# Forgetting attention and a gated feed-forward: a joined score bank, weights in three chunks, additive masks for batch 0, and a new stored order

## The chip, the cores and the metric

One core of a Trainium2 chip runs the whole kernel in one launch. The engines work side by side: PE (TensorE, matrix products and transposes), DVE (VectorE), ACT (ScalarE), POOL (GpSimd) and SP (SyncE, which issues transfers here). Each follows its own stream of instructions, and they meet at semaphores. The metric is the time of one execution on the device, in microseconds (us); lower is better.

## What is computed

There are B = 8 batches, H = 8 heads, S = 576 positions, head size D = 64. The attention decays with distance: the score of query i and key j has the sum of the logarithms of the forget gates between them added. Its output, 4608 rows of 512, goes through a root-mean-square norm and a gated feed-forward of width 1536.

```python
scores = scale * np.matmul(q, k.transpose(0, 1, 3, 2))
cum = np.cumsum(np.log(np.clip(f, 0.0001, 1.0)), axis=-1)
scores = np.where(causal, -1e9, scores + cum[..., :, None] - cum[..., None, :])
attn = softmax(scores); x = (attn @ v) as rows of H * D
xn = x / np.sqrt(np.mean(x * x, axis=-1, keepdims=True) + 1e-06) * rms_g
g = xn @ w_gate
out = (g * sigmoid(g) * (xn @ w_val)) @ w_out
```

(The second line and the line of the softmax are shortened.)

## The kernel before

The kernel is a list of small *pieces*, each a few instructions for one engine, registered by `plan.add` under a name. The string ORDER, stored at the top of the file, names all of them in one sequence. `Plan.run` walks it and issues each piece to its engine; so ORDER sets the order within each engine, and the engines run apart as far as data and buffers allow. `*n` after a name asks for n filler matmuls (L235, `warm_up`) that compute nothing, ahead of that piece's own; `:ff` picks the PSUM pool for a product of values.

The decay isn't added to scores. The exponential of minus the cumulated gates is folded into V and into a 65th column of V that collects the denominator, so a division at the end gives the attention.

The names, where b is a batch, p one of four pairs of heads, g a group of rows:

- `Lq`, `Lk`, `Lqk`, `Lv` (L388 to L400, L431) load 256 KB pieces of q, k and v (128 or 64 KB for the last 64 rows), all from SP's queue. `Cq`, `Ck`, `Cqk` (L412) cast them to bf16, nearly all on POOL. `Sv` (L419 to L426) scales v.
- `tr`, `trt` (L491 to L521) turn q and k on PE in batches 0 to 2; `keeptr` (L508, L513, L524) copies the result out of PSUM. `tk`, `tq`, `tt` (L552, L555) are DMA transposes from batch 3 on.
- `sc` (L620) computes one or two banks of scores of a pair into a tile of 2 × 512 columns (two heads side by side), of which there are two. `esc` (L628) takes the exponential on ACT into a tile PT, and `msc` (L636) zeroes the part above the diagonal on POOL. `k4`, `sc4`, `exp4`, `mask4` (L580, L589, L593, L597) do the last 64 rows.
- `val` (L656) multiplies by V; `xpo` (L665, L666) divides by the denominator into x. `sq` (L673, ACT), `ms` (L679, DVE), `rs` (L684, POOL) and `xn` (L688, DVE) are the norm. `xtr`, `kxtr` (L715 to L724) turn x on PE in batches 0 and 1; `tx` (L707) does so by DMA later.
- `g`, `v` with a suffix f (L811) are the gate and value matmuls, `th` (L816) a tanh on ACT, `ga`, `hga` (L820, L827) the gating on DVE, `pj` (L837) the projection in two parts, `o` (L842) the copy out of PSUM, `so` (L845) the store, from POOL's queue except in the last group.
- `wg`, `wv` (L352, four chunks each) and `wo` (L364, two) load the weights from POOL's queue.

The rows are taken in ten groups: two of 256 rows (g0, g1), then eight of 512. The first 256 positions of batch 0 are a part of their own (HEAD), so that g0 can begin; the rest of batch 0 (REST) has three banks a pair, and batches 1 to 7 (WHOLE) three banks a pair with all 576 positions. Each bank is a list of blocks: (key block, first query, queries, column in the tile).

Buffers: 10 for loads, 6 for cast operands, 4 PT, two score tiles, one PSUM bank for values, three PSUM banks `ff` shared by gate, value, projection and transposes. ORDER puts the feed-forward of a group among the attention of the batches that follow.

Of the kernel before, what the change touches and what calls it, by code (L numbers as in the profile page):

```python
# [16 lines left out]
NB = 5  # L17
# [17 lines left out]
g0.6 exp4.1 Lk2.0 hga0.4 sc1.0.1024 keeptr1.3.q th0.6 xtr0.3 Lq2.3 v0.6f ga0.6 kxtr0.3 xn0.4 esc1.1.0 xtr0.2 Lqk20 g0.8 kxtr0.2 hga0.6 g1.0 th0.8
esc1.0.1024 ga0.8 v1.0f Sv1.0 Lk2.1 th1.0 sc1.1.512 ga1.0 g1.2 esc1.1.1024 Lq2.0 hga1.0 v0.8f th1.2 esc1.1.512 Lk2.3 ga1.2 g0.10 hga0.8 v1.2f
msc1.1.1024 th0.10 ga0.10 sc1.2.0 mask4.1 esc1.2.0 xtr0.4 g1.4 Sv1.4 kxtr0.4 hga1.2 esc1.2.512 v1.4f th1.4 msc1.0.1024 Lq2.1 v0.10f ga1.4 Sv1.2
sc1.2.1024 hga1.4 g1.6 esc1.3.0 hga0.10 Sv1.3 v1.6f th1.6 esc1.2.1024 ga1.6 g1.8 Lqk21 Sv1.1 v1.8f th1.8 ga1.8 sc1.3.512 esc1.3.512 val1.0.0 hga1.6
Lk2.2 val1.1.0:ff hga1.8 esc1.3.1024 g1.10 pj0.0.0 msc1.3.1024 th1.10 ga1.10 msc1.2.1024 Lv2.3 xpo1.1.0 Lv2.41 xpo1.0.0 val1.2.0:ff Ck2.0 val1.4.0:ff
xpo1.2.0 Lv3.41 pj0.0.0e Cq2.0 xpo1.4.0 val1.5.0 o0.0.0 val1.3.0:ff Ck2.1 Lq2.2 xpo1.5.0 val1.6.0:ff Ck2.3 Lk3.0 xpo1.3.0 tr2.0 Cq2.1 val1.7.0 Lqk31  # L40
xpo1.6.0 keeptr2.0.k Cqk2 tr2.1 Lk3.3 keeptr2.0.q pj0.1.0 Cq2.3 keeptr2.1.k Lq3.3 xpo1.7.0 keeptr2.1.q sq1.1 Lv2.40 Sv2.3 sq1.2 Lq3.0 pj0.1.0e so0.0.0
v1.10f o0.1.0 Ck2.2 Lq3.1 sq1.4 trt2 sc2.0.0 keeptrt2 sq1.0 Cq2.2 hga1.10 tr2.3 Lqk30 sq1.3 k4.2 tr2.2 pj1.0.0 Lv2.0 ms1.0 keeptr2.2.k keeptr2.2.q
rs1.0 esc2.0.512 keeptr2.3.q Lq3.2 keeptr2.3.k xn1.3 sc4.2 pj1.0.0e xn1.0 exp4.2 xtr1.3 o1.0.0 pj1.1.0 xn1.1 kxtr1.3 xn1.2 esc2.0.0 xn1.4 xtr1.0
xtr1.1 kxtr1.0 pj1.1.0e kxtr1.1 xtr1.2 sc2.0.1024 kxtr1.2 Cq3.0 esc2.0.1024 xtr1.4 g2.0 kxtr1.4 tq3.0 o1.1.0 Cq3.1 v2.0f th2.0 Cqk3 esc2.1.0 Lv2.1
ga2.0 g2.1 Cq3.3 tq3.1 hga2.0 Ck3.3 v2.1f th2.1 Ck3.0 ga2.1 sc2.1.512 Lv2.2 mask4.2 esc2.1.512 g2.2 hga2.1 Lq4.3 msc2.0.1024 v2.2f tk3.0 th2.2 Sv2.0
esc2.1.1024 ga2.2 g2.3 Lk4.0 hga2.2 Cq3.2 v2.3f th2.3 Lk3.1 Sv2.1 ga2.3 sc2.2.0 tt3 g2.4 esc2.2.512 hga2.3 Sv2.2 tq3.2 v2.4f th2.4 Sv2.4 esc2.2.0
# [85 lines left out]
class Plan:  # L132
# [779 lines left out]
```

The softmax here doesn't subtract the row's maximum and nothing guards it: scores larger than these inputs give would overflow.

## Time and profile before

| | us |
|---|---|
| median of 5 executions | 384.13 |
| lowest and highest | 382.42, 384.77 |
| the profiled execution, its own time | 384.13 |
| its span, first to last instruction | 382.1 |
| ACT, all exponentials of scores (L628) | 96.8 |
| PE, gate and value matmuls (L811) | 110.1 + 109.7 |
| PE, projection (L837) | 97.2 |
| POOL, casts (L412) | 43.9 |
| POOL, masks (L636) | 37.6 |
| POOL, store issues (L845) | 18.4 |

The span is what the trace covers; 2.0 us of the profiled execution's own time lie outside it. Matmuls overlap in PE's pipeline, so the sum of their durations is somewhat above the time in which PE works. The busy time of an engine says how full it is, and not whether anything waited for it.

### The profile page before, as it was taken

What the parts mean: (1) busy time and instruction counts of PE and PEld (TensorE: products, weight loads), DVE (VectorE), ACT (ScalarE), POOL (GpSimd) and SP (SyncE); (2) the same over time, 40 slices, a digit from 0 to 9 for tenths busy, and PEclk for the clock granted to TensorE, in tenths of its full rate; (3) what the DMA queues carried; (4) which work ended last, traced back from release to release, by engine and by line L of the source; (5) the groups of instructions that cost most, each with busy time, mean ns of one, the idle gap of its engine ahead of it and who ended that gap; (6) DMA issues with size and microseconds to landing.
All of it is one profiled execution on the core that took longest, in us unless ns stands there. A gap on an engine that the chain in (4) does not pass through costs nothing.

```text
span 382.1 us, 8426 instructions
## 1 busy us (share of the span) xinstructions
PE 366.3 (96%) x3270; PEld 203.3 (53%) x3314; DVE 246.4 (64%) x460; ACT 215.0 (56%) x357; POOL 174.3 (46%) x281
## 2 busy tenths in 40 slices
PE   8679899989999999999999999999999999999996
PEld 7457787744654644454445544554444544444443
DVE  4656875776777776467855877487348845743750
ACT  2667786578687568346655496556554353313322
POOL 4667626878398537793664359224111221001000
PEclk9989999999999999999999999999999999999999
DMA  8999997799779999999997964830001224022002
GB/s 204 187 260 236 233 237 161 166 205 174 165 159 221 157 190 196 207 197 179 222 171 121 205 143 102 118 107 13 14 30 21 84 69 98 1 62 84 0 6 107
DMA packets 144840, 52.62 MB, mean 138 GB/s; under 512 B 128220, under 2 KB 142304, under 8 KB 144800
## 3 DMA queue, kind: packets, MB, share of 16 engines
q1 hardware_dynamic: 136336, 38.82, 53.7%
q0 software_dynamic: 8384, 13.11, 15.1%
q8 instruction: 26, 0.43, 0.5%
q10 hardware_dynamic: 80, 0.15, 0.1%
q14 instruction: 14, 0.11, 0.1%
HBM read 37.90 MB, written 9.44 MB: 124 GB/s over the span
## 4 chain that ended last, share of the span: by engine, by line
PE 85%; DVE 5%; ACT 4%; DMA 3%; SPq 2%; issue 1%; ACTq 0%; DVEq 0%
PE ff L811 49%; PE ff L837 22%; PE sc L620 6%; PE po L656 4%; PE ff L656 3%; DMA st<-in_v_dram 2%; ACT junk L673 1%; DVE xn L688 1%; DVE x L666 1%; ACT PT L628 1%; SPq L431 1%; DMA xT<-xn 1%; ACT QK L513 1%; DVE QK L513 1%; PE sc L235 1%
## 5 line engine op out<-in xcount | busy, mean ns | idle before, releaser
L820 DVE SCALAR_TENSOR_TENSOR ga<-th,ff 128x512 f32<-128x512 f32 x108 | 74.1, 686 | 66.6 <-ACT th L816 65.0
L628 ACT ACTIVATE PT<-sc 128x1024 bf16<-128x1024 f32 (+2 forms) x100 | 96.8, 990 | 29.8 <-PE sc L620 29.8
L811 PE MATMUL ff<-xT,wg 128*128 128x512 bf16 (+1 forms) x467 | 110.1, 357 | 1.0 <-DMA xT<-xn 0.2
L811 PE MATMUL ff<-xT,wv 128*128 128x512 bf16 (+1 forms) x464 | 109.7, 357 | 0.8
L816 ACT ACTIVATE th<-ff 128x512 f32<-128x512 f32 x108 | 64.5, 597 | 72.6 <-PE ff L811 67.4
L837 PE MATMUL ff<-wo,hT 128*128 128x512 bf16 (+1 forms) x429 | 97.2, 373 | 0.7
L827 DVE SCALAR_TENSOR_TENSOR hT<-ga,ff 128x512 bf16<-128x512 f32 x108 | 73.8, 685 | 7.9 <-PE ff L811 0.2
L636 POOL TENSOR_SCALAR_AFFINE_SELECT PT<-PT 128x1024 bf16<-128x1024 bf16 (+1 forms) x44 | 37.6, 865 | 77.0 <-ACT PT L628 76.3
L811 PEld LDWEIGHTS <-wg 128*128 128x128 bf16 x480 | 44.7, 98 | 43.4 <-issue 1.9
L811 PEld LDWEIGHTS <-wv 128*128 128x128 bf16 x480 | 45.1, 98 | 42.4 <-issue 1.0
L837 PEld LDWEIGHTS <-hT 128*128 128x128 bf16 x444 | 42.2, 98 | 46.4 <-issue 1.1
L412 POOL CAST ld<-st 128x512 bf16<-128x512 f32 x68 | 43.9, 668 | 24.5 <-DMA st<-in_q_dram 9.7
L842 ACT COPY ores<-ff 128x512 f32<-128x512 f32 (+1 forms) x37 | 21.0, 574 | 48.6 <-PE ff L837 41.4
L688 DVE SCALAR_TENSOR_TENSOR xn<-x,rs,rgb 128x512 bf16<-128x512 f32 x40 | 37.2, 959 | 6.9 <-POOL rs L684 6.8
L656 PEld LDWEIGHTS <-PT 128*128 128x128 bf16 x896 | 33.5, 98 | 12.3 <-issue 2.9
L845 POOL DMA_DIRECT2D out_dram<-ores x32 | 18.4, 576 | 39.6 <-ACT ores L842 39.6
L419 POOL TENSOR_TENSOR Vs<-st,decT 128x512 bf16<-128x512 f32 x27 | 29.0, 1076 | 9.4 <-DMA st<-in_v_dram 9.0
L620 PE MATMUL sc<-QK 64*128 64x128 bf16 (+2 forms) x328 | 28.6, 270 | 1.2 <-DVE QK L508 1.0
L673 ACT ACTIVATE junk<-x 128x512 bf16<-128x512 f32 x40 | 25.1, 628 | 3.1 <-DVE x L666 2.6
L620 PEld LDWEIGHTS <-QK 64*128 64x128 bf16 x584 | 15.8, 95 | 18.4 <-issue 13.3
L656 PE MATMUL po<-Vs,PT 128*128 128x65 bf16 x521 | 22.3, 194 | 1.8 <-DVE Vs L420 1.8
L666 DVE TENSOR_TENSOR x<-po,rden 128x320 f32<-128x320 f32 (+2 forms) x39 | 18.6, 478 | 1.3
(84 smaller groups left out, 232.0 us busy)
## 6 DMA issues: line engine op xcount, KB each, us to landing
st<-in_k_dram SPq DMA_DIRECT2D x32, 256.0 KB, 4.7
st<-in_q_dram SPq DMA_DIRECT2D x32, 256.0 KB, 4.4
st<-in_v_dram SPq DMA_DIRECT2D x32, 256.0 KB, 4.4
out_dram<-ores POOLq DMA_DIRECT2D x32, 256.0 KB, 3.0
wo<-in_moe_w_out_dram POOLq DMA_DIRECT2D x2, 768.0 KB, 14.2
st<-in_k_dram SPq DMA_DIRECT2D x8, 128.0 KB, 4.5
st<-in_q_dram SPq DMA_DIRECT2D x8, 128.0 KB, 5.6
st<-in_v_dram SPq DMA_DIRECT2D x16, 64.0 KB, 4.3
```

Of the source, the lines that this page charges most:

```text
L412: {"DVE": nc.vector.tensor_copy, "POOL": nc.gpsimd.tensor_copy, "ACT": nc.scalar.copy}[eng](o, x)
L419: e.tensor_tensor(Vs[i][:, j, :, 0:D], t, bcast(dj, D), ALU.mult)
L620: nc.tensor.matmul(sc[:, par, c:c + n], lhsT=k_cols(r, p, kj), rhs=q_cols(r, p, q0, n), start=True, stop=True)
L628: nc.scalar.activation(T["pt", b, p][:, :, c0:c0 + n], T.pop(("sc", b, p, c0))[:, :, 0:n], ACT.Exp, scale=scale)
L636: nc.gpsimd.affine_select(out=d, in_=d, pattern=[[0, m], [1, 128]], compare_op=ALU.is_ge, fill=0.0, base=0, channel_multiplier=-1)
L656: nc.tensor.matmul(T["po", b, hs][:, qm, m, :], lhsT=w, rhs=Vs[i][:, kj, h, :], start=(kj == 0), stop=(kj == qi))
L688: nc.vector.scalar_tensor_tensor(xn, in0=T["x", b][:, j, :], scalar=T["rs", b, js][:, j:j + 1], in1=rgb, op0=ALU.mult, op1=ALU.mult)
L811: nc.tensor.matmul(ps[:, c * w:c * w + w], lhsT=wt[:, dc, (fc + c) * 128:(fc + c + 1) * 128], rhs=T["xT", g][:, dc, 0:w], start=(dc == 0), ...
L816: nc.scalar.activation(t, T["pg", g, fc], ACT.Tanh, scale=0.5)
L820: nc.vector.scalar_tensor_tensor(a, in0=T.pop(("th", g, fc)), scalar=1.0, in1=T.pop(("pg", g, fc)), op0=ALU.add, op1=ALU.mult)
L827: nc.vector.scalar_tensor_tensor(o, in0=T.pop(("ga", g, fc)).rearrange("p (c t) -> p c t", t=w), scalar=0.5, in1=T.pop(("pv", g, fc)).rear ...
L837: nc.tensor.matmul(po, lhsT=T["hT", g][:, fc, j * 128:(j + 1) * 128], rhs=wo[:, fc, c0:c1], start=(fc == 0), stop=(fc == NFC - 1))
```

## The change

*Joined bank.* The blocks of key block 0 in batches 1 to 7, of 128 and 384 queries, become one of 512; that bank is computed first (suffix 512), and the one of suffix 0 after it.

*Masks.* For batch 0, `msc` goes. A piece `far` opens the PSUM tile with a product of the identity and a constant triangle of −30000, and the score matmuls add to it. For batches 1 to 7, one select over 1024 columns becomes three.

*Batch 0's last small banks* (suffix 384) of all four pairs share one score tile and one visit.

*Weights* come in three chunks per matrix. *x* has fixed tiles with one more column that holds a constant, so that the square's sum has the epsilon in it, and `ms` goes. *Fillers* go in runs of 512 columns, and their number is another: 176 of 128 columns before, 81 units of 128 after.

*Engines.* A mark `@` in ORDER names the engine of a piece (A is ACT, D DVE, O POOL, S SP). 24 casts go to ACT and 13 to DVE; 16 loads are issued by ACT instead of SP; 12 output copies go to DVE; of the stores, 8 go to ACT, 11 to SP and three of the last group to POOL; four of the eight `k4` leave POOL.

*Dependence.* `expo` and every `esc` now follow `fetch`, the piece that fetches the exponential's table.

*Order.* The whole string is another. Below it is cut to the head, up to the first gate piece, and to the start of the last group.

```diff
-one lf ident Lk0.0 Lq0.1 rg identb clear Lk0.1 Lq0.0 Lq0.2 Lqk11 Lk0.2 clip turn_rg*48 keep_rgT Lqk00 Ck0.0 fetch_ln spread_rg*3 Lv0.0 Cq0.1 log scan
-Lv0.1 Cq0.0 Ck0.1 tr0.01*29 tr0.00 Cq0.2 Lk0.3 keeptr0.00.k keeptr0.00.q keeptr0.01.k expo Lqk01 keeptr0.01.q tr0.02*7 sc0.1.0 keeptr0.02.q Lv0.40
-esc0.1.0 twice keeptr0.02.k Lq0.3 Ck0.2 sc0.2.0*5 msc0.1.0 turn_dec esc0.2.0 Lv0.3 sc0.0.0 tr0.03 keep_rg msc0.2.0 keeptr0.03.k Lk1.0 keeptr0.03.q
-Lv0.41 keep_dec sc0.3.0*8 wv0 tr0.10 esc0.3.0 Sv0.1 Lq1.0 wg1 esc0.0.0 Ck0.3 Lv1.40 Sv0.0 fetch msc0.0.0 Lv0.2 keeptr0.10.q val0.2.0*16 Lk1.2 xpo0.2.0
-msc0.3.0 val0.0.0:ff*5 sc0.1.512 xpo0.0.0 val0.4.0 esc0.1.512 Cqk0 xpo0.4.0 val0.6.0:ff Cq0.3 xpo0.6.0 Lq1.2 Ck1.0 tr0.12*8 Lk1.1 sq0.1 sc0.0.512 wg0
-Lq1.3 keeptr0.12.q keeptr0.10.k trt0 sq0.0 keeptrt0 sc0.3.512*1 esc0.3.512 ms0.0 rs0.0 keeptr0.12.k sc0.2.512*10 wv1 xn0.0 esc0.2.512 Sv0.3 wg2
-sc0.1.1024*10 k4.0 xn0.1 Lq1.1 xtr0.0 esc0.1.1024 Lqk10 tri esc0.0.512 kxtr0.0 Lv1.41 xtr0.1*9 Sv0.2 sc0.2.1024 Cq1.0 kxtr0.1 sc4.0 Sv0.4 esc0.2.1024
-Lk1.3 g0.0*1 msc0.1.1024 Lv1.0 sc0.0.1024 th0.0 v0.0f exp4.0 ga0.0 esc0.0.1024 sc0.0.384 g0.2 mask4.0 hga0.0 esc0.0.384 msc0.0.1024 sc0.1.384 tr1.0
...
-hga8.6 v8.7f th8.7 ga8.7 g8.8 hga8.7 v8.8f th8.8 ga8.8 g8.9 hga8.8 v8.9f th8.9 ga8.9 g8.10 hga8.9 v8.10f th8.10 ga8.10 g8.11 hga8.10 v8.11f th8.11
-xn7.4 pj8.0.0 ga8.11 tx7.4.9 xn7.1 hga8.11 tx7.1.9 pj8.0.0e pj8.1.0 o8.0.0 tx7.3.9 so8.0.0 pj8.1.0e pj8.2.0 pj8.2.0e pj8.3.0 o8.2.0 o8.1.0 so8.2.0
...
+one lf far Lq1.0 Lq0.0 Lq0.1@A ident Lk0.0 Lv0.1@A tri identb clear Lk0.1 Lq0.3@A fetch_ln rg Lk0.2 clip Lk0.3@A log Cq0.1@A scan Lq0.2 Cq0.0@A Lqk01
+fetch Lv0.0 Ck0.0 tr0.01*48 Lqk11@A far0.1.0 keeptr0.01.q tr0.00 keeptr0.01.k far0.3.0 expo keeptr0.00.q sc0.1.0 Ck0.1@D Cq0.3@A twice keeptr0.00.k@D
+tr0.02 Lv0.40 turn_dec esc0.1.0 Lk1.0 tr0.03 turn_rg Ck0.2@O Lqk00@A far0.0.0 keeptr0.03.q keep_rgT keeptr0.03.k sc0.0.0 Lqk10@A Ck0.3 sc0.3.0
+keeptr0.02.k tr0.12 esc0.3.0 keep_dec Lq1.3 Cq0.2 keeptr0.02.q Sv0.1@O Lv0.2@A tr0.10*2 keeptr0.12.q far0.1.1024 esc0.0.0 keeptr0.12.k@D spread_rg
+Cq1.0 Lv0.3 keeptr0.10.k Cqk0@D far0.2.0 keeptr0.10.q sc0.2.0 Lk1.3@A Sv0.0@O trt0 esc0.2.0 Lv0.41 keeptrt0 wv0 sc0.1.1024*6 Cqk1@A val0.0.0 Lk1.2
+val0.4.0:ff keep_rg val0.6.0:ff xpo0.0.0 k4.0 Lk1.1 esc0.1.1024 val0.2.0:ff sc0.0.384 Lq1.2 wg0 xpo0.2.0 esc0.1.384 Lq1.1 sc4.0 xpo0.4.0 wg1 exp4.0
+xpo0.6.0 esc0.3.384 far0.3.1024*4 esc0.0.384 Ck1.0 esc0.2.384 sc0.3.1024 Sv0.2 sq0.0 sc0.1.512 Lv1.41 trt1 esc0.3.1024 keeptrt1 Lv1.40 Sv0.3@O
+esc0.1.512 Lqk20 sc0.0.512*9 Sv0.4 Lqk21 sq0.1 far0.0.1024*2 wv1 sc0.0.1024 esc0.0.512 rs0.0 Lk2.0 esc0.0.1024 sc0.2.512*6 tr1.0 mask4.0 xn0.1
+far0.2.1024 keeptr1.0.q@A k4.1 Lv1.0 sc0.2.1024 esc0.2.512 keeptr1.0.k@D val0.0.2 val0.1.2:ff xpo0.0.2 esc0.2.1024 sc0.3.512 Cq1.2@O xpo0.1.2 val0.2.2
+xn0.0 Ck1.1 esc0.3.512 val0.5.2:ff val0.3.2:ff xpo0.5.2 xtr0.0 wg2 sc1.0.512 Cq1.1@A kxtr0.0 xpo0.3.2 esc1.0.512 xtr0.1 Cq1.3 val0.4.2:ff xpo0.2.2
+val0.6.2:ff wv2 Lq2.0 xpo0.4.2 kxtr0.1 val0.7.2 xpo0.6.2 Ck1.3@O tr1.1 esc1.0.0 xpo0.7.2 sc4.1 Ck1.2 g0.0 Lv1.3 keeptr1.1.k@D sq0.2 keeptr1.1.q v0.0f
...
+th8.6 ga8.6 g8.7 hga8.6 v8.7f th8.7 ga8.7 g8.8 hga8.7 v8.8f th8.8 ga8.8 g8.9 hga8.8 v8.9f th8.9 ga8.9 g8.10 hga8.9 v8.10f th8.10 ga8.10 g8.11 hga8.10
+g9.0 th8.11 ga8.11 v9.0f th9.0 ga9.0 g9.1 hga9.0 v8.11f th9.1 pj8.0.0 hga8.11 ga9.1 pj8.0.0e v9.1f o8.0.0@D g9.2 hga9.1 pj8.1.0 th9.2 ga9.2 pj8.1.0e
+v9.2f o8.1.0 pj8.2.0 hga9.2 so8.1.0 pj8.2.0e g9.3 o8.2.0 v9.3f so8.2.0@S th9.3 so8.0.0@S ga9.3 g9.4 hga9.3 v9.4f th9.4 ga9.4 g9.5 hga9.4 pj8.3.0 th9.5
...
+def words():
+    for word in ORDER.split():
+        word, _, fill = word.partition("*")
+        word, _, pool = word.partition(":")
+        name, _, eng = word.partition("@")
+        yield name, eng, pool, int(fill or 0)
+
+
+ON = {name: {"A": "ACT", "D": "DVE", "O": "POOL", "S": "SP"}[eng] for name, eng, _, _ in words() if eng}
...
 WHOLE = (
-    (0, ((0, 384, 128, 0), (0, 0, 384, 128)), None),
-    (512, ((1, 128, 384, 0), (3, 384, 128, 384)), None),
-    (1024, ((0, 512, 64, 0), (1, 512, 64, 64), (2, 512, 64, 128), (3, 512, 64, 192), (2, 256, 256, 256)),
-     (128, 384, 4)),
+    (512, ((0, 0, 512, 0),), None),
+    (0, ((1, 128, 384, 0), (3, 384, 128, 384)), None),
+    (1024, ((0, 512, 64, 0), (1, 512, 64, 64), (2, 512, 64, 128), (3, 512, 64, 192), (2, 256, 256, 256)), True),
 )
-HEAD = ((0, ((0, 0, 256, 0), (1, 128, 128, 256)), (0, 256, 2)),)
+HEAD = ((0, ((0, 0, 256, 0), (1, 128, 128, 256)), True),)
 REST = (
     (512, ((0, 256, 256, 0), (1, 256, 256, 256)), None),
-    (1024, ((0, 512, 64, 0), (1, 512, 64, 64), (2, 256, 256, 128), (3, 384, 128, 384)), (1152, 256, 2)),
+    (1024, ((0, 512, 64, 0), (1, 512, 64, 64), (2, 256, 256, 128), (3, 384, 128, 384)), True),
     (384, ((2, 512, 64, 0), (3, 512, 64, 64)), None),
 )
 
...
     def warm_up(ps):
-        for _ in range(st.pop("fill", 0)):
-            nc.tensor.matmul(ps[:, 0:128], lhsT=idle, rhs=idle, start=True, stop=True)
+        k = st.pop("fill", 0)
+        for w in [4] * (k // 4) + [1] * (k % 4):
+            x = bass.AP(tensor=idle.tensor, offset=idle.offset, ap=[idle.ap[0], [0, w], [1, 128]])
+            nc.tensor.matmul(ps[:, 0:w * 128], lhsT=idle, rhs=x, start=True, stop=True)
...
+        for t in X:
+            nc.vector.memset(t[:, :, DM:], 1e-3 * DM ** 0.5)
...
+    def make_far():
+        nc.gpsimd.memset(far, 0.0)
+        nc.gpsimd.affine_select(out=far, in_=far, pattern=[[1, 256]], compare_op=ALU.is_ge, fill=-30000.0, base=0,
+                                channel_multiplier=-1)
...
-    p_exp = plan.add("expo", "ACT", 0.78, expo, [p_scan])
+    p_exp = plan.add("expo", "ACT", 0.78, expo, [p_scan, p_pre])
...
-    WCH = ((0, 256), (256, 512), (512, 1024), (1024, 1536))
+    WCH = ((0, 256), (256, 768), (768, 1536))
...
+        def ring(eng):
+            return nc.scalar if eng == "ACT" else nc.sync
+
+        def load_rows(nm, src, j, eng):
+            ring(eng).dma_start(out=stage((nm + "s", b, j)).rearrange("p (h d) -> p h d", d=D),
                               in_=src[b, :, j * 128:(j + 1) * 128, :].rearrange("h p d -> p h d"))
...
+        def open_sc(p, c0):
+            sc = T["sc", b, p, c0] = ps_sc.tile([128, 2, 512], F32, name="sc", tag="sc")
+            warm_up(sc[:, 0, :])
+            return sc
+
+        def far_first(p, bank):
+            sc = open_sc(p, bank[0])
+            diag = [(n, c) for kj, q0, n, c in bank[1] if q0 == kj * 128]
+            for par in range(2):
+                for m, (n, c) in enumerate(diag):
+                    nc.tensor.matmul(sc[:, par, c:c + n], lhsT=ident, rhs=far[:, 0:n], start=(m == 0), stop=False)
+
         def scores(visit):
-            for p, (c0, blocks, _) in visit:
-                sc = T["sc", b, p, c0] = ps_sc.tile([128, 2, 512], F32, name="sc", tag="sc")
-                warm_up(sc[:, 0, :])
+            if len(visit) == NP:
+                sc = open_sc(0, visit[0][1][0])
+                for p, bank in visit:
+                    T["sc", b, p, bank[0]] = sc[:, :, p * 128:p * 128 + 128]
+            for p, bank in visit:
+                c0, blocks, _ = bank
+                opened = bank[2] and ("sc", b, p, c0) in T
+                sc = T["sc", b, p, c0] if ("sc", b, p, c0) in T else open_sc(p, c0)
+                st.pop("fill", 0)
                 for kj, q0, n, c in blocks:
                     for par in range(2):
                         r = slice(par * 64, par * 64 + 64)
                         nc.tensor.matmul(sc[:, par, c:c + n], lhsT=k_cols(r, p, kj),
-                                         rhs=q_cols(r, p, q0, n), start=True, stop=True)
+                                         rhs=q_cols(r, p, q0, n), start=not opened,
+                                         stop=not opened or (kj, q0) == blocks[-1][0:2])
 
         def exps(p, bank):
             c0, blocks, _ = bank
...
         def mask(p, bank):
-            c, step, n = bank[2]
             pt = T["pt", b, p]
-            runs = [(0, 2 * n)] if step * n == 1536 else [(0, n), (1, n)]
-            for par, m in runs:
-                d = bass.AP(tensor=pt.tensor, offset=pt[:, par, c:].offset, ap=[pt.ap[0], [step, m], [1, 128]])
-                nc.gpsimd.affine_select(out=d, in_=d, pattern=[[0, m], [1, 128]], compare_op=ALU.is_ge, fill=0.0,
-                                        base=0, channel_multiplier=-1)
+            for par, c, step, n in ((0, 0, 384, 2), (1, 0, 384, 2), (0, 512, 768, 4)):
+                d = bass.AP(tensor=pt.tensor, offset=pt[:, par, c:].offset, ap=[pt.ap[0], [step, n], [1, 128]])
+                nc.gpsimd.affine_select(out=d, in_=d, pattern=[[0, n], [1, 128]], compare_op=ALU.is_ge, fill=0.0, base=0,
+                                        channel_multiplier=-1)
...
-            nc.scalar.activation(junkp.tile([128, DM], BF16, name="junk"), T["x", b][:, j, :], ACT.Square,
+            nc.scalar.activation(junkp.tile([128, DM + 1], BF16, name="junk"), X[i][:, j, :], ACT.Square,
                                  scale=DM ** -0.5, accum_out=T["sq", b, js][:, j:j + 1])
-
-        def mean(js):
-            a, z = js[0], js[-1] + 1
-            ms = T["ms", b, js] = small.tile([128, NB], F32, name="ms")
-            nc.vector.tensor_scalar(ms[:, a:z], in0=T["sq", b, js][:, a:z], scalar1=1e-6, op0=ALU.add, scalar2=None)
...
+            visits = [ps[u:u + each] for u in range(0, len(ps), each)]
+            if banks is REST:
+                visits = [[(p, bank)] for p in range(NP) for bank in banks[0:2]] + [[(p, banks[2]) for p in range(NP)]]
...
+                far_on = split and visit[0][1][2]
+                if far_on:
+                    p, bank = visit[0]
+                    a = plan.add(f"far{b}.{p}.{bank[0]}", "PE", 0.26, lambda p=p, bank=bank: far_first(p, bank), [p_far, p_idb],
+                                 acq=[("sc", keys[0])], kind="A")
+                    deps.append(a)
...
-            ms = plan.add(f"ms{b}.{js[0]}", "DVE", 0.12, lambda: mean(js), sq)
-            rs = plan.add(f"rs{b}.{js[0]}", "POOL", 0.8 if now else 0.9, lambda: rstd(js), [ms, p_id])
+            rs = plan.add(f"rs{b}.{js[0]}", "POOL", 0.8 if now else 0.9, lambda: rstd(js), sq + [p_id])
...
-        def keep_o(j, c0, c1):
+        def keep_o(j, c0, c1, eng):
             o = T["o", g, j, c0] = orp.tile([128, DM], F32, name="ores", tag="ores")
-            nc.scalar.copy(o[:, 0:c1 - c0], T.pop(("pj", g, j, c0))[:, 0:c1 - c0])
-
-        def store(j, c0, c1):
-            (nc.sync if end else nc.gpsimd).dma_start(out=out[t0 + j * 128:t0 + (j + 1) * 128, c0:c1],
+            copy(eng, o[:, 0:c1 - c0], T.pop(("pj", g, j, c0))[:, 0:c1 - c0])
+
+        def store(j, c0, c1, eng):
+            {"SP": nc.sync, "ACT": nc.scalar, "POOL": nc.gpsimd}[eng].dma_start(out=out[t0 + j * 128:t0 + (j + 1) * 128, c0:c1],
                                                       in_=T.pop(("o", g, j, c0))[:, 0:c1 - c0])
```

## The prediction

> **What bounds the kernel now.** I read the page's shares, then its slices, the shares of the chain of waits, a table of windows, and PE's timeline inside the poor window. The shares, the slices and the chain's shares by engine:
>
> ```profile
> PE 366.3 (96%) x3270; PEld 203.3 (53%) x3314; DVE 246.4 (64%) x460; ACT 215.0 (56%) x357; POOL 174.3 (46%) x281
> ...
> PE   8679899989999999999999999999999999999996
> ...
> PE 85%; DVE 5%; ACT 4%; DMA 3%; SPq 2%; issue 1%; ACTq 0%; DVEq 0%
> ```
>
> PE (TensorE) is busy 96% of the 382.1 us, and clearly short only in the second, third and fifth slice of 9.55 us and in the last. So the kernel is a full PE stream behind a head. Three stretches of that head (columns: busy us of PE, its weight loads, DVE, ACT, POOL; granted PE clock; DMA share; GB/s):
>
> ```profile
> 0.00:10.00 10.00, 7.99 (x95) 7.57 (x96) 4.73 (x16) 3.12 (x6) 4.41 (x13) 1.00 0.91 202
> 10.00:20.00 10.00, 6.95 (x114) 5.42 (x114) 6.98 (x20) 6.24 (x9) 6.38 (x12) 1.00 1.10 185
> 20.00:30.00 10.00, 7.14 (x88) 5.34 (x86) 5.95 (x17) 6.92 (x13) 6.71 (x12) 0.83 1.23 265
> ```
>
> And what PE does there (start, duration, what; in brackets the idle time before and who ended it):
>
> ```profile
> 17.92 0.34 PE L656 MATMUL po<-Vs,PT 128*128 128x65 bf16 x6 [1.76 <-DVE Vs L420]
> ...
> 23.45 0.72 PE L235 MATMUL sc<-idle 128*128 128x128 bf16 x10 [1.61 <-ACT PT L628]
> ...
> 25.61 1.23 PE L235 MATMUL sc<-idle 128*128 128x128 bf16 x10 [1.12 <-ACT PT L628]
> ```
>
> The first values wait for V (its DMA lands at 15.42, and DVE scales it), then the second half of batch 0's scores waits for exponentials on ACT. Lines of L235 are filler matmuls that compute nothing. The first gate matmul, g0.0, is at 29.91 us, by the same timeline. From there PE is dense: 96 gate and value matmuls run from 316.55 to 337.11, 0.2157 us each. The last matmul ends at 378.75; copy and store take 3.3 us more.
>
> **What the Trainium skill says.** "TensorE: Matmul & The Clock Gate", Part 1, gives a warm 512-column matmul 215.7 ns, with 2.5 ns of it fixed; the trace's 0.2157 agrees, so one matmul for two saves some 2.5 ns. The same part halves the clock after an idle window of about 3.4 us; here the granted clock is 0.83 at 20–30 us, beside idles of only 1.61 and 1.12. It also calls ACT's queue strictly first in, first out; no view of before tests a waiting load on ACT. "DMA: Bandwidth & Descriptors", Issuing engines are not separate DMA queues: loads put on ACT share the same 16 engines with SP's, so they save issue time only; the DMA share of 0.91 to 1.23 in the windows agrees that the head has no bandwidth to spare.
>
> **The change, by parts.**
>
> *One 512 bank.* 28 pair-banks with two 128-column and two 384-column matmuls become two of 512: 56 matmuls fewer, the columns the same. 56 × 2.5 ns = 0.14 us of PE. Weight loads run beside matmuls. As good as nothing.
>
> *Masks.* A diagonal mask of batches 1–7 is one select of 1024 columns now, and three (256, 256, 512) after. By shape, L636 has 1.10 us for 1024 (28 of them) and 0.45 us for 256 (16); the line through both gives 0.67 for 512, so 1.57 for 1.10: 28 × 0.47 = 13 us more on POOL over the run. POOL is busy 46% and loses 34 of its 68 casts of 0.67 us (23 us) and 16 of 32 store issues of 0.58 us (9 us), so it ends lighter. At most the values of a pair come 0.5 us later: other PE work stands ahead of them; 0 taken, 0.5 us per batch as upper end. Batch 0's 16 masks leave POOL (7.2 us of the head) for 32 matmuls that add −30000 above the diagonal, 16 × 128 and 16 × 256 columns: 2.6 us of PE, all in a head where PE idles or runs filler (176 filler matmuls of 128 columns, 9.5 us at 0.2157 per 512, become some 10,500 columns, 4.4 us). Cost 0; 2.6 if the head is PE-bound, which the windows deny.
>
> *Small terms.* Batch 0's last small banks share one score buffer and one visit of 16 matmuls of 64 columns: its first exponential waits for all four pairs, some 0.3 us longer, and three turns of the two buffers are saved; below 0.5 us either way, 0 taken. Weights in three chunks: 8 issues become 6, 2 × 0.77 us of POOL, but the first wide chunk lands later. wg0 is needed at g0.0 and issued near 22; eight us suffice. The eps column removes nine adds, one DVE hop of 0.2 us ahead of each rstd; a group's x is normally ready well ahead: 0 to −0.2 once, in the head. wo1, now issued at 45.64, landing at 61.97 and wanted at 65.36, will be issued near 56 and land near 63, wanted at 67.6: cover 4 us.
>
> *The order, the main term.* Now 40 gate and value matmuls of g0 (256 columns) lie among batch 0's second half and batch 1's first score banks; after, all of batch 0's attention, tr1.0, tr1.1, sc1.0.512 and sc4.1 stand before g0.0. So g0.0 comes later, and less is left behind it. What is left on PE in before from v0.4f (44.80) on: 1188 matmuls × 0.2157 = 256.3; 176 of 256 columns × 0.109 = 19.2; 56 value visits × 0.45 = 25.2; 41 score visits × 0.55 = 22.6; transposes 4 × 0.45 and 8 × 0.23 = 3.6; small ones 1.1. Sum 327.9, against 333.95 elapsed: 6.0 us are lost to stalls and joints. In after from g0.0: the same with 216 of 256 columns (23.5) and 6 × 0.45: 333.2. With the same 6.0 lost: 339.2. So before's end is matched by g0.0 at 378.75 − 339.2 = **39.5 us**.
>
> When is g0.0? Loads up to v0's last rows are 3.36 MB; at the 202 and then 185 GB/s of the windows this is 10 + 1.34/0.185 = 17.2 us; with the landing behind it and weights between, 18.5. ACT's order holds loads Lqk00, Lqk10, Lv0.2 and Lk1.3 between exponentials; each needs a buffer or DMA slot that earlier landings free, the last some time near 18.5. So ACT's head exponentials end near 20.7 (in before 16.3, by ACT's timeline). Then ACT's own list, at the pitches that its timeline shows (0.92 us for 1024 columns, 0.72 for 768, 0.3 for 256, 0.72 with its read for a square): to sq0.1 6.8 us (27.5); six more exponentials and one keep, 5.2 us (32.7); Cq1.1, esc1.0.512, kxtr0.1, 2.1 (34.8). Then tr1.1 and sc4.1, 0.6 and joints: g0.0 at **35.9**. PE's own list (values, far, scores: some 12 us of work from 18.5, an estimate from the same rows) is shorter, so ACT bounds this stretch. Gain 39.5 − 35.9 = 3.6.
>
> *Behind g0.0.* Work by stage, PE/ACT/DVE, each listed piece at the duration of its row: to pj0.0.0 31.6/26.3/27.7 us, so PE still bounds; from pj1 to g2.6 19/19.5 (18.2/15 in before), since casts and keeps move to ACT: no loss taken, up to 3 us. Later ACT is at 75% of PE or less. Twelve output copies go to DVE, and ten V scalings while four leave it (64% busy); four of the eight pairs of copies of the last rows' keys (1.36 us a pair in before) leave POOL for ACT and DVE: all counted in these sums.
>
> *The end.* g9's first gates stand before g8's last projections: the pause of about 0.4 us at group 8's projection goes. The last projection, copy and store stay: −0.4. Stores issued by POOL instead of SP: ±0.3.
>
> Sum: −3.6 − 0.4 = −4.0 on the profiled execution's own 384.13 (2.0 outside the span), which is also the median: **380.2 us** with rounding of the small terms.
>
> **Rivals.**
>
> A, the head is shorter still: ACT's loads do not wait, head exponentials end by 18, and ACT's list starts 2.5 us earlier: 377.6. For: before ended them at 16.3 with the same bandwidth, and the exponential's table (1.28 us on ACT at 9.70 in before, with the decay waiting behind it) is fetched ahead now. Against: V still lands no sooner than in the sum, and one load of batch 1 now goes first (256 KB, 1.3 us at 202 GB/s).
>
> B, ACT becomes the bound from pj1 to g2.6 and gives back 3 us: 383. For: 19.5 against 19 us is no slack. Against: this stage's casts can run ahead.
>
> C, slower: ACT stands in its loads. Each of the four waits for the landing of an earlier transfer, with exponentials behind it in a strict queue, and PE's scores behind those (two score buffers). If the landings come at the pace of 160 to 170 GB/s that later slices of the page show instead of 185 to 202, the last comes 3 us later, and a second clock drop like before's adds 2: g0.0 at 42.5 instead of 35.9, 387. It decides from g0.0 at 41.4 on (39.5 + 1.9). For: ACT issues one load in before and 16 after. Against: SP, relieved, issues its own sooner.
>
> D, it does nothing: the order moves work about, PE-bound at both places, within 0.5%. The idle and filler of the head (over 15 us of it) speak against it.
>
> **How the numbers follow.** Chances: the sum as it stands 0.48, A 0.19, B 0.12, D 0.04, C 0.17. 0.5% (1.9 us) is about what a measurement of this kernel can tell from no change. B and D at 383 to 384 are mostly within it, of the sum's case a little: faster 0.68, same 0.14, slower 0.18. The range takes in A's far end (both head and later stalls shrink: 376.3) and C's near half, 386.2; 0.1 is left on either side. The likeliest case alone: 378.5 to 382.
>
> **What would show it.** g0.0 between 34.5 and 37.5; ACT busy nearly throughout 20–35; filler under 5 us; masks of L636's place at about 0.45, 0.45 and 0.67 in triples; from g0.0 to the last matmul 339 ± 1.5; one pause less near group 8's projection. It is wrong if g0.0 passes 39.5, if a wait of ACT's queue on DMA above 2 us stands in the head, or if PE idles over 1 us between pj1 and g2.6.

## The result and the profile after

The changed kernel takes 381.54 us (median of 26 executions, 379.69 to 383.78), the kernel before 383.58 us (47 executions, 382.18 to 386.65). The ratio is 0.9941, with a 95% interval of 0.9926 to 0.9956: about 2 us faster, half of the 4 us that were forecast. That it is faster is clear of the noise; that it is faster by more than 0.5% is not, since the interval runs from 0.44 to 0.74%. The execution that was profiled took 383.30 us, at the slow end of its kernel; its span is 381.6 us.

The page of the changed kernel, in the lines that were shown of before: shares, PE's slices with the granted clock, and the shares of the chain of waits by engine.

```profile
PE 365.9 (96%) x3097; PEld 196.1 (51%) x3138; DVE 260.3 (68%) x497; ACT 220.3 (58%) x369; POOL 136.0 (36%) x249
...
PE   4969999999999999999999999999999999999996
...
PEclk9589999999999999999999999999999999999999
...
PE 71%; DMA 8%; issue 6%; ACT 5%; POOL 4%; DVE 4%; SPq 0%; POOLq 0%; ACTq 0%
```

It is still a full PE stream behind a head. POOL went from 46 to 36%, as the parts said. New is the second digit of PE's clock: half speed for nearly a slice. The windows of the head (columns as above: busy us of PE, weight loads, DVE, ACT, POOL; clock; DMA share; GB/s):

```profile
0.00:10.00 10.00, 5.10 (x17) 1.96 (x18) 4.13 (x15) 4.21 (x6) 3.52 (x15) 0.88 0.90 220
10.00:20.00 10.00, 9.55 (x80) 6.95 (x79) 6.16 (x17) 5.33 (x10) 4.90 (x8) 0.60 1.28 223
20.00:30.00 10.00, 7.11 (x96) 4.13 (x96) 5.19 (x18) 8.29 (x17) 6.00 (x10) 0.83 1.26 251
```

The 9.55 busy us of the second window are no gain over 6.95 before: at clock 0.60 the same work lasts longer (the eight transposing matmuls of tr0.12 take 1.03 us here, at 15.89, and 0.62 us at full clock in a later run, e2). PE's timeline says where it began, and when the first gate matmul comes (start, duration, what; in brackets the idle before and what ended it):

```profile
1.09 4.32 PE L253 MATMUL ff<-idle 128*128 128x512 bf16 x12 [1.09 <-DVE idle L265]
9.02 0.40 PE L540 MATMUL ff<-ident,ld 128*128 128x128 bf16 x2 [3.61 <-ACT ld L222]
...
22.84 0.34 PE L714 MATMUL ff<-Vs,PT 128*128 128x65 bf16 x6 [1.32 <-ACT rgb L222]
...
38.01 1.04 PE L863 MATMUL ff<-xT,wg 128*128 128x256 bf16 x8
```

The filler, now a few wide matmuls, is done at 5.41 us; the first cast of q is late; PE idles 3.61 us. g0.0 is at 38.01. And the chain of waits up to 24 us, cut to its larger pieces (start, length, what):

```profile
1.32 3.93 DMA st<-in_q_dram
...
5.27 9.10 DMA st<-in_q_dram
...
14.39 7.23 DMA st<-in_q_dram
...
21.68 0.62 ACT ld L222
22.30 0.48 ACT rgb L222
22.79 0.93 ACT PT L688
```

The third step is a load of q's last rows of batch 1 (Lqk10), issued by ACT at 14.39 when an earlier load had landed. ACT's cast of it (Cqk1) waits until 21.64, and the first exponential of batch 0's second half stands behind that cast.

### The profile page after: what moved, and what is told of

Its sections match the earlier page's. It is cut to its first block, busy times and chain, and to the rows that moved or that the text cites. A ratio compares the mean times of both kernels' runs of the same rounds, so it can differ in the third digit from the quotient of the medians.

```text
span 381.6 us, 8127 instructions
## 1 busy us (share of the span) xinstructions
PE 365.9 (96%) x3097; PEld 196.1 (51%) x3138; DVE 260.3 (68%) x497; ACT 220.3 (58%) x369; POOL 136.0 (36%) x249
## 4 chain that ended last, share of the span: by engine, by line
PE 71%; DMA 8%; issue 6%; ACT 5%; POOL 4%; DVE 4%; SPq 0%; POOLq 0%; ACTq 0%
PE ff L863 42%; PE ff L889 19%; DMA st<-in_q_dram 6%; PE sc L679 4%; PE po L714 3%; ACT PT L688 2%; DVE xn L739 2%; POOL PT L694 1%; PE ff L714 1%; DVE X L722 1%; DMA out_dram<-ores 1%; POOL rs L735 1%; ACT junk L729 1%; ACT th L868 1%; DMA st<-in_v_dram 1%
## 5 line engine op out<-in xcount | busy, mean ns | idle before, releaser
L694 POOL TENSOR_SCALAR_AFFINE_SELECT PT<-PT 128x256 bf16<-128x256 bf16 (+1 forms) x84 | 42.7, 534 | 73.9 <-ACT PT L688 73.7
L739 DVE SCALAR_TENSOR_TENSOR xn<-X,rs,rgb 128x512 bf16<-128x512 f32 x40 | 34.0, 874 | 8.9 <-POOL rs L735 8.8
L897 POOL DMA_DIRECT2D out_dram<-ores x16 | 9.2, 578 | 68.2 <-ACT ores L222 36.0
L222 ACT COPY ores<-ff 128x512 f32<-128x512 f32 (+1 forms) x25 | 14.2, 568 | 33.0 <-PE ff L889 27.6
L222 POOL CAST ld<-st 128x512 bf16<-128x512 f32 x34 | 21.7, 646 | 26.6 <-DMA st<-in_k_dram 15.3
L679 PE MATMUL sc<-QK 64*128 64x256 bf16 (+3 forms) x272 | 28.9, 299 | 0.3 <-ACT QK L222 0.2
L735 POOL TENSOR_TENSOR rs<-sq,mhalf 128x5 f32<-128x5 f32 (+2 forms) x9 | 9.9, 1104 | 51.9 <-ACT junk L729 51.9
L729 ACT ACTIVATE junk<-X 128x513 bf16<-128x513 f32 x40 | 25.4, 635 | 3.9 <-DVE X L722 3.4
L451 POOL TENSOR_TENSOR Vs<-st,decT 128x512 bf16<-128x512 f32 x22 | 23.4, 1063 | 8.2 <-DMA st<-in_v_dram 6.6
L679 PEld LDWEIGHTS <-QK 64*128 64x128 bf16 x528 | 13.7, 96 | 17.9 <-issue 13.3
```

Source lines behind the costliest of these rows:

```text
L222: {"DVE": nc.vector.tensor_copy, "POOL": nc.gpsimd.tensor_copy, "ACT": nc.scalar.copy}[eng](o, x)
L679: nc.tensor.matmul(sc[:, par, c:c + n], lhsT=k_cols(r, p, kj), rhs=q_cols(r, p, q0, n), start=not opened, stop=not opened or (kj, q0) == b ...
L694: nc.gpsimd.affine_select(out=d, in_=d, pattern=[[0, n], [1, 128]], compare_op=ALU.is_ge, fill=0.0, base=0, channel_multiplier=-1)
L729: nc.scalar.activation(junkp.tile([128, DM + 1], BF16, name="junk"), X[i][:, j, :], ACT.Square, scale=DM ** -0.5, accum_out=T["sq", b, js] ...
L739: nc.vector.scalar_tensor_tensor(xn, in0=X[i][:, j, 0:DM], scalar=T["rs", b, js][:, j:j + 1], in1=rgb, op0=ALU.mult, op1=ALU.mult)
```

## The experiments

All ratios are to runs of the kernel before that were taken beside them on the same chip; "the changed kernel" is 0.9941 from its 26 executions. g0.0 is the start of the first gate matmul in a run's one profiled execution, and "behind g0.0" is from there to the end of the last matmul: 340.2 us in the changed kernel's profile, against 338.8 in the forecast (339.2, and 0.4 less at the end).

**e1, the changed kernel again.** No edit.

> The changed kernel, unaltered, on the chip of the next three, as their yardstick. Both theories: 380 to 383 us, half clock on PE again from about 8 to 17 us in the profile, g0.0 between 35.5 and 38.5 us.

381.81 us (380.16 to 382.84), ratio 0.9931 (0.9907 to 0.9954). Half clock from 8.4 to 18.7 us, g0.0 at 36.77, behind it 340.9. So one kernel's g0.0 moves by over 1 us between executions, and single profiles are read here for mechanisms, not for sizes.

**e2, filler until the first cast.**

```diff
-tr0.01*48
+tr0.01*112
```

> The filler ahead of the first transpose grows from 48 to 112 units (16 more matmuls of 512 columns, 3.5 us), so that PE has work from 5.4 us until the first cast of q is there at about 9 us. Theory CLOCK (the granted clock at one half from 7.8 to 17.5 us is what the head lost): the clock stays at 1.00 there, g0.0 comes 1.5 to 2.5 us earlier, and the time is 1.5 to 2.5 us below the yardstick. Theory ACT (ACT's own queue, with loads and a cast that wait for landings in it, sets the head): the clock is repaired too, but g0.0 and the time move by less than 0.5 us.

382.41 us, ratio 0.9951 (0.9932 to 0.9970): no gain. The clock was held, then fell later. The first two lines are windows of the changed kernel, the next two of e2:

```profile
16.00:20.00 4.00, 3.79 (x38) 3.26 (x38) 2.75 (x7) 2.60 (x4) 3.68 (x6) 0.76 1.24 227
20.00:24.00 4.00, 1.97 (x52) 1.58 (x52) 1.73 (x8) 2.61 (x5) 3.29 (x6) 1.00 1.30 236
```

```profile
16.00:20.00 4.00, 1.83 (x36) 1.23 (x35) 1.98 (x6) 1.14 (x2) 3.81 (x7) 1.00 1.24 241
20.00:24.00 4.00, 2.70 (x37) 1.76 (x38) 2.56 (x9) 3.81 (x10) 2.31 (x4) 0.50 1.28 252
```

PE, done sooner with its early work, waits between 16 and 20 us (busy 1.83 of 4), and the half clock now falls on the scores between the exponentials. Theory CLOCK, in its plain form, falls.

**e3, four loads back on SP.**

```diff
-Lqk00@A ... Lqk10@A ... Lv0.2@A ... Lk1.3@A
+Lqk00 ... Lqk10 ... Lv0.2 ... Lk1.3
```

> Four loads of the head (Lqk00, Lqk10, Lv0.2, Lk1.3) go back from ACT's queue to SP's, at the same places of the order. Theory ACT: exponentials of the first part are free of them and g0.0 comes 1 us or more earlier, time 1 us or more below the yardstick. Theory CLOCK: within 0.5 us of the yardstick. A third outcome, that SP's queue delays the loads behind them, would show as 1 us or more slower.

382.65 us (22 executions, 380.71 to 386.00), ratio 0.9968 (0.9946 to 0.9989). Not faster, by the medians 1 us slower. Taking these loads off ACT, the mechanism of rival C, brings nothing here; e3 leans to the third outcome, though the intervals touch.

**e4, the cast Cqk1 behind the small exponentials.**

```diff
-sc0.1.1024*6 Cqk1@A val0.0.0 ... esc0.2.384 sc0.3.1024
+sc0.1.1024*6 val0.0.0 ... esc0.2.384 Cqk1@A sc0.3.1024
```

> The cast Cqk1 on ACT, which in the profile of the changed kernel waits 1.38 us for a load's landing with an exponential behind it, goes behind the small exponentials of batch 0. Theory ACT: those exponentials start 1.3 us earlier, g0.0 and the time gain 0.8 to 1.3 us on the yardstick. Theory CLOCK: the exponentials start earlier, and wait for scores or norm instead; within 0.5 us of the yardstick.

381.29 us, ratio 0.9923 (0.9897 to 0.9949); g0.0 at 35.23. The first exponential of the second half starts at 20.55 instead of 22.69. The gain of about 0.5 us on e1 lies within the intervals: by itself unclear.

**e5, both, and filler where e2 idled.** e4's edit, e2's, and `trt0*24`.

> The later cast of e4, the longer filler of e2, and 24 more units of filler ahead of the transposes of the last rows (trt0), where e2 let PE idle 1.33 us and its clock fell at 20 us instead of 8. Theory LIST (ACT's list of exponentials sets the head, and PE's clock counts only where a score stands between two of them): full clock to 30 us, ACT's list begins near 18.5 and runs its 14 us, g0.0 at 33.5 to 34.5, time 379.3 to 380.5. Theory LANDING (transfers set the start of that list): g0.0 stays at 35 or later and the time at 381 to 382, whatever the clock is.

380.19 us (379.35 to 381.30), ratio 0.9909 (0.9888 to 0.9931). The clock of this execution is 1.00 throughout. The window of 20 to 30 us and g0.0, in e5:

```profile
20.00:30.00 10.00, 7.57 (x128) 4.77 (x125) 7.46 (x20) 9.31 (x18) 8.10 (x13) 1.00 1.25 247
```

```profile
34.02 1.04 PE L863 MATMUL ff<-xT,wg 128*128 128x256 bf16 x8
```

ACT is busy 9.31 of 10 us there (8.29 in the changed kernel): its list runs almost without holes, as theory LIST had it, with time and g0.0 inside its numbers. But e4, without the fillers, has the same 9.31. What the fillers add to e4 is that the head's exponentials end earlier, at 18.01 instead of 20.18. And this g0.0 is one profile's: e9 below has the same edits in the head and g0.0 at 35.66.

**e11, e5's fillers without the later cast.**

> The two fillers of e5 without its later cast, the missing corner of four (none 381.8, cast alone 381.3, both 380.2). Theory LIST: clock and cast each give a part, ACT's list begins where the load of Lqk10 lands (near 19.7 us) and runs 14 us at full clock: g0.0 at 34 to 35, time 380.5 to 381.3. Theory CLOCK ALONE: 380.2 as e5. Theory CAST ALONE: 381.6.

381.79 us, ratio 0.9938 (0.9912 to 0.9964): the last of the three outcomes, no gain. PE still waited 1.31 us for ACT behind Cqk1 (the copy of the norm's weights frees a PSUM bank), and the clock was 0.50 in the window from 24 to 28 us. With e1, e4 and e5 this makes the four corners: 0.9931 with neither, 0.9938 with the fillers, 0.9923 with the cast, 0.9909 with both. The fillers alone move the slow stretch; the cast alone is unclear; both together are the best of the four, though their interval meets e1's.

**e6, four output buffers.** In the changed kernel and in e1 to e4, PE stops near 125 us, by 0.34 to 0.90 us. The changed kernel's line of it, then e2's:

```profile
126.52 0.58 PE L714 MATMUL ff<-Vs,PT 128*128 128x65 bf16 x14 [0.34 <-ACT ores L222]
```

```profile
125.59 0.58 PE L714 MATMUL ff<-Vs,PT 128*128 128x65 bf16 x14 [0.90 <-ACT ores L222]
```

PE waits for an output copy on ACT, this for an output buffer, and this for stores; POOL issued them here (timeline of POOL in e2), behind the three selects of a mask and a scaling of V:

```profile
116.19 2.26 POOL L694 TENSOR_SCALAR_AFFINE_SELECT PT<-PT 128x256 bf16<-128x256 bf16 x3 [0.73 <-ACT PT L688]
118.41 1.48 POOL L451 TENSOR_TENSOR Vs<-st,decT 128x512 bf16<-128x512 f32 x1
119.83 0.41 POOL L452 CAST Vs<-decT 128x8 bf16<-128x8 f32 x1
120.16 1.17 POOL L897 DMA_DIRECT2D out_dram<-ores  x2
```

```diff
-pool("orp", 3)
+pool("orp", 4)
```

> Four output buffers instead of three. In all five profiles of the changed kernel and its variants PE stops 0.5 to 1.1 us near 125 us: values wait for a PSUM bank, this for an output copy on ACT, this for a store that POOL issued late, behind three selects of one mask (2.25 us). Theory MASK (the three-part mask cost this stop): it goes, time 0.5 to 1.0 us below 381.6. Theory NONE: the stop moves on to the next wait, below 0.3 us.

381.32 us, ratio 0.9924 (0.9905 to 0.9942), which cannot be told from the changed kernel. Its profile has the stop at the next piece instead, and longer:

```profile
125.91 0.81 PE L863 MATMUL ff<-xT,wg 128*128 128x512 bf16 x3 [1.91 <-issue]
```

An output copy on ACT still waited for a store, which landed at 123.8 us; what PE waited for after that copy, the profile doesn't name.

**e9, e5 with these two stores on ACT.**

```diff
-so2.1.0 ... so1.1.0
+so2.1.0@A ... so1.1.0@A
```

> e5 with the stores so1.1.0 and so2.1.0 issued by ACT, at the same places of the order, instead of POOL, where they stand behind the three selects of a mask. e6 only moved the stop near 125 us (from the values to the first gate of group 3, 1.91 us) since its fourth buffer still waited for the same late stores. Theory MASK-STORE: with the stores issued early no stop over 0.3 us is left between 120 and 127 us, and the time is 0.3 to 1 us below e5's 380.2. Theory NONE: something else holds group 3's first gate there; within 0.3 us of e5.

380.26 us, ratio 0.9913 (0.9889 to 0.9937). The two output copies on ACT ahead of group 3, in e5 and then in e9 (in brackets the idle before and what ended it):

```profile
121.88 1.23 ACT L222 COPY ores<-ff 128x512 f32<-128x512 f32 x2 [1.72 <-DMA out_dram<-ores]
```

```profile
122.99 1.22 ACT L222 COPY ores<-ff 128x512 f32<-128x512 f32 x2 [1.39 <-PE ff L889]
```

In e5 they wait for a store to land, in e9 only for their projection: the edit took the wait for the store away. For PE this was worth little here: from 120 to 127 us it is busy 6.95 of 7 us in e9, and already 6.88 in e5, which has the late stores. So the edit shows what held the copies, and not what the longer stops of the changed kernel and e1 cost. Behind g0.0 e9 takes 339.7 us, against 340.2 in e5 and in the changed kernel and 340.9 in e1. The time is e5's: a part of 0.5 us can't be seen in these medians, and in this profile a half-clock stretch came back in the head (g0.0 at 35.66).

**e7, the joined bank and its masks alone, in the kernel before.**

```diff
-    (0, ((0, 384, 128, 0), (0, 0, 384, 128)), None),
-    (512, ((1, 128, 384, 0), (3, 384, 128, 384)), None),
+    (512, ((0, 0, 512, 0),), None),
+    (0, ((1, 128, 384, 0), (3, 384, 128, 384)), None),
...
+            runs = [(0, 0, 384, 2), (1, 0, 384, 2), (0, 512, 768, 4)] if step * n == 1536 else [(0, c, step, n), (1, c, step, n)]
```

(with the suffixes 0 and 512 of `sc` and `esc` exchanged in batches 1 to 7.)

> The kernel before with only the joined 512 bank and the three-part masks of batches 1 to 7, in its old order. By the prediction: 0.1 us gained on PE, the 13 us more on POOL hidden: 0 within 0.5 us of before. Rival: POOL, which in the old order still does 68 casts and 32 stores, makes masks late: 1 to 3 us slower than before.

Ratio 1.0000 (0.9988 to 1.0013): nothing, as forecast.

**e8, batch 1's load behind those of batch 0.**

```diff
-one lf far Lq1.0 Lq0.0 ... scan Lq0.2 Cq0.0@A
+one lf far Lq0.0 ... scan Lq0.2 Lq1.0 Cq0.0@A
```

> The load Lq1.0 of batch 1, first in SP's queue in the changed kernel, goes behind Lq0.2, as far as its cast allows. Theory LANDING: all loads of batch 0 land about 1 us earlier (256 KB at 220 GB/s is 1.2 us), ACT's first cast and g0.0 too, time 0.7 to 1.2 us below 381.6. Theory LIST: ACT's list begins earlier by less than half of that; below 0.5 us.

382.95 us (22 executions, 380.51 to 385.86), ratio 0.9969 (0.9950 to 0.9987): no gain, by the medians 1 us slower. Its profiled execution was one of the quick ones (380.74 us, g0.0 at 35.26), so the profile doesn't show what the others lost. Why it spreads so, as e3 does, stays open.

**e10, the additive triangles undone in the changed kernel.** Batch 0's masks are selects on POOL again, behind the exponentials.

```diff
-                far_on = split and visit[0][1][2]
+                far_on = False
...
+            if split:
+                c = 0 if bank[0] == 0 else 1152
+                runs = ((0, c, 256, 2), (1, c, 256, 2))
```

(`far0.*` leaves ORDER, and `msc0.*` stands behind the last `esc` that it covers.)

> The changed kernel with batch 0's additive triangles undone: the 32 products of the identity go, and batch 0's masks are selects on POOL again, two of 256 columns each behind the exponential. By the prediction (cost and gain of the additive form both hidden): within 0.5 us of 381.6. Rival HELPS: masks on POOL stand in front of the scaling of V and the weights' issues there, and the values wait for them: g0.0 1 us or more later, time 0.8 to 2 us above 381.6. Rival HURTS: 2.6 us of products at full clock, more at half, were on the path: 0.8 us or more below.

383.51 us, ratio 0.9997 (0.9981 to 1.0013): the whole gain is gone. PE's timeline of e10 has a stop that the changed kernel doesn't have:

```profile
33.73 0.45 PE L718 MATMUL ff<-Vs,PT 128*128 128x65 bf16 x9 [1.15 <-POOL PT L698]
```

Values wait for a mask on POOL. Earlier in the head PE waits 1.12 us for a cast that POOL makes late, and 0.71 us for its copy of the last rows' keys. But g0.0 of this profile, 37.35, is no later than the changed kernel's 38.01 and 0.6 us later than e1's, so theory HELPS has its time and not its g0.0. Other places for these masks, earlier in POOL's order or on another engine, were not tried.

**e12, the triangles alone, in the kernel before.** The same edit the other way: `far` pieces directly ahead of their scores, no `msc0`.

> The kernel before, in its old order, with batch 0's masks on POOL replaced by the additive triangles alone (each far piece directly ahead of its scores). e10 lost 1.9 us by undoing them in the changed kernel. Theory PART (the triangles are worth about 2 us by themselves, since values no longer wait for POOL): 1 to 2 us below before. Theory ORDER (they are worth it only where all of batch 0's values stand close behind its exponentials, as in the new order; in the old order gate matmuls lie between): within 0.5 us of before. Below nothing: 2.6 us of products on PE in a dense stretch after g0.0 (half of them stand there) would make it 0.5 to 1.3 us slower.

385.17 us, ratio 1.0026 (1.0009 to 1.0042): slower, by about 1 us, the outcome named last. In its profile the clock of 20 to 30 us is 0.70 (0.83 before) and g0.0 comes at 31.81 instead of 29.91.

## Why the forecast held, and where it was off

**The main term.** The sum gave g0.0 at 35.9, from a list on ACT that begins when the head's exponentials end, "near 20.7", and runs 14.1 us. Those exponentials ended at 20.31 in the changed kernel and at 20.57 in e1, so the number came out, but not by its reason. The forecast had them stand behind loads in ACT's queue that wait for landings. In the changed kernel (first two lines) the last waits were for scores, and PE computed these at half clock; in e2 (next two), with full clock to 20.0 us, the exponentials were done at 17.65, and what held the list then was the cast Cqk1:

```profile
16.00 0.81 ACT L688 ACTIVATE PT<-sc 128x768 bf16<-128x768 f32 x1 [2.23 <-PE sc L679]
...
19.50 0.81 ACT L688 ACTIVATE PT<-sc 128x768 bf16<-128x768 f32 x1 [0.88 <-PE sc L679]
```

```profile
16.84 0.81 ACT L688 ACTIVATE PT<-sc 128x768 bf16<-128x768 f32 x1 [0.86 <-PE sc L679]
19.67 0.62 ACT L222 CAST ld<-st 128x512 bf16<-128x512 f32 x1 [2.02 <-DMA st<-in_q_dram]
```

At full clock waits behind loads do come up (1.02 us in e5, 2.15 in e11), and yet the exponentials ended between 17.65 and 19.09 (e2, e5, e9, e11). So rival A was nearer on how they run, and that 20.7 was met is luck: half clock, which the sum didn't have, filled the place.

The list's first piece is Cqk1. It was counted without a wait for its load, which landed at 21.62; it began at 21.68 in the changed kernel and 21.66 in e1. This is the first term that was mis-sized: 1.0 us. From there to the end of its last copy (kxtr0.1) the list took 15.7 us in the changed kernel's profile and 14.5 in e1, which has full clock from 18.7 us on. Of the 1.2 us between the two, some 0.5 had come by the copy at 31.15 (30.68 in e1), with a second stretch of half clock from 24.8 to 28.2 before it. The other 0.8 came from the norm: the second scaling (xn) on DVE took 1.68 us in the changed kernel (first line) and 0.74 in e1 (second), and in the changed kernel a transposition on PE waited for it, and an exponential on ACT for the scores behind that (last two):

```profile
33.34 1.68 DVE L739 SCALAR_TENSOR_TENSOR xn<-X,rs,rgb 128x512 bf16<-128x512 f32 x1
```

```profile
32.86 0.74 DVE L739 SCALAR_TENSOR_TENSOR xn<-X,rs,rgb 128x512 bf16<-128x512 f32 x1
```

```profile
35.08 0.40 PE L766 MATMUL ff<-ident,xn 128*128 128x128 bf16 x4 [0.60 <-DVE xn L739]
```

```profile
35.90 1.02 ACT L688 ACTIVATE PT<-sc 128x1024 bf16<-128x1024 f32 x1 [0.91 <-PE sc L679]
```

This scaling took 1.47 to 1.68 us in the profiles of the changed kernel, e2, e9 and e11, and 0.74 in those of e1, e4, e5, e6 and e8. What stretches it was not tested. The joint behind the list took 0.6 us instead of 1.1. In e4 and e5, with the cast moved and none of these waits, the list takes 14.1 us from its first exponential to that copy, close to the forecast's 14.1, which counted a copy of some 0.5 us ahead of it too. e5's g0.0 of 34.02 and time of 380.19 are where the forecast's 380.2 is, by way of more edits.

**The clock.** The forecast counted fewer fillers as cost 0, with the head's idle as cover, and named a clock drop only inside rival C. It came: 10.2 us of half speed, from 7.7 to 17.9. It held the head's exponentials back by up to 2.7 us (20.31, 17.65 in e2), most of which the landing of Cqk1's load covered. e2 and e11 show that more filler alone isn't the cure: the slow stretch came back later, among the scores of the list. The Trainium skill ("TensorE: Matmul & The Clock Gate", Part 1) puts the drop after an idle window of about 3.4 us. Here it came 2.3 us into an idle of 3.61 us, and e2's drop at 20 us had no idle above 1.33 us before it, only 2.2 us of idle within 4. Shorter idles than the page's were enough, and the measurement decides.

**The triangles.** They were booked as an exchange at cost 0 and gain 0. e10 says that they are worth about what the whole change is worth, and e12 that they cost 1 us in the old order. Both fit one reading, which is argued: in the old order gate matmuls stand between batch 0's exponentials and its values, which covers the masks; in the new one the values follow closely, and a mask on POOL would hold them. As tested here, the new order pays only with the triangles, and the triangles only with the new order. The forecast's total had both in it, so this was an error of attribution, not of the sum. That the order without triangles, with the masks where e10 puts them, is worth nothing is shown; that its head is what makes them needed rests on stops of 1.15, 1.12 and 0.71 us in one profile, whose g0.0 isn't late.

**Behind g0.0.** Forecast 338.8 us, measured 340.2 and 340.9. Of the missing 1.4 to 2.1 us, some 0.5 is the tail (below), and 0.34 in the changed kernel and 0.68 in e1 is the stop near 125 us, traced to stores behind masks on POOL. The forecast bounded the masks by "0.5 us per batch" and took them as 0. The rest is spread in pieces below 0.4 us, and was not traced.

**The tail.** The forecast took 0.4 us off for a pause at group 8's projection. Before has no such pause; its 48 projections there take 10.36 us, 0.2158 each:

```profile
337.11 10.52 PE L837 MATMUL ff<-wo,hT 128*128 128x512 bf16 x48
347.47 1.03 PE L811 MATMUL ff<-xT,wg 128*128 128x512 bf16 x3
```

From g8's first gate matmul to the end of the last matmul it is 62.5 us in the changed kernel (315.74 to 378.23) and 62.4 before (316.39, which the forecast read as 316.55, to 378.74), so nothing was gained there.

**The small terms.** Selects were put at 0.45 and 0.67 us and took 0.47 (56 of 256 columns) and 0.67 (28 of 512). Bank and masks: e7, nothing, in the old order. Rival B: in the window from 80 to 100 us ACT is busy 17.3 of 20 us (14.3 before) and PE 19.6 (18.9 before): crowded, without loss. Rival C: e3 took four of the loads off ACT and gained nothing; its 42.5 for g0.0 is also 1.6 us more than its own parts, 3 and 2 on 35.9, give. One cover was thinner than said: the second half of the projection's weights was issued at 57.47 and landed at 68.25, 1.6 us ahead of the first projection at 69.82, not 4. Of the signs, g0.0 between 34.5 and 37.5 holds in e1 (36.77) and not in the changed kernel's profile (38.01), and 339 ± 1.5 behind it holds in the changed kernel's profile (340.2) and just not in e1 (340.9).

**A version that is likely faster still.** e5 and e9 stand at 0.9909 and 0.9913 of before, about 3.4 us, against 0.9941 and 0.9931 for the changed kernel. Two kernels that share the edits agree; the intervals overlap a little, so the further 1 us is likely and not proven.

## What to carry to other kernels

When an engine's list of instructions is summed, each piece that consumes a transfer is to be put at the later of its turn and its landing; here one early cast in ACT's queue held a microsecond of exponentials. A start time that comes out right is no proof of its reason: ask which wait ended last. Filler matmuls are worth what stands behind them: ask which engine sets the pace in that stretch, before a clock is bought. And a change made of an order and of the operations that the order needs is tested as a whole and each way round: here each half alone was worth nothing or less.

## What the runs showed of the hardware that wasn't expected

Half clock can outlast dense work: in the changed kernel's profile PE was busy in all of 12 to 17 us, and the clock stayed at 0.50 until 17.9. The window of 12 to 16 us (busy PE, weight loads, DVE, ACT, POOL; clock; DMA share; GB/s):

```profile
12.00:16.00 4.00, 4.00 (x32) 2.44 (x33) 2.22 (x8) 1.78 (x3) 1.23 (x2) 0.50 1.35 187
```

Where the slow stretch falls moved from one execution to the next and with small edits (7.7 to 17.9 and 24.8 to 28.2 us in the changed kernel, 8.4 to 18.7 in e1, 20.0 to 26.8 in e2, none in e5). Their lengths come in steps: by windows of 0.1 us the half-clock stretches in the head last 3.4, 6.8, 10.2 or 13.7 us, multiples of about 3.41, in all 13 profiles that have one (before, the changed kernel and the variants). In the 3.4 us ahead of these 15 drops PE was busy for some 20 to 53% of the time. One and the same scaling on DVE took 0.74 us in some profiles and up to 1.68 in others. Executions of one kernel spread over 4.1 us here (379.69 to 383.78), and those of before over 4.5, so effects of half a microsecond need more than the six executions that half of these runs had.
